# Gated linear attention and a cosine-gated MLP on one core: another hand-written order of the same steps

## The chip, the cores and the metric

One core of a Trainium2 chip runs the whole program. The metric is the device time of one execution in microseconds (us), the median of a few runs. The profiler recorded one execution; all times inside it count from the first instruction of the program.

## The reference

Four batches of eight heads, 768 positions, 48 values a head. A state of 48 x 48 decays row by row and takes an outer product at every position; the queries read it. The result, 3072 rows of 384, goes through a two-layer MLP whose hidden values are multiplied by their cosine.

```python
def _attn_ref(q, k, v, alpha):
    for t in range(S):
        state = alpha[:, :, t, :, None] * state + np.einsum('bhd,bhe->bhde', k[:, :, t], v[:, :, t])
        y[:, :, t] = np.einsum('bhd,bhde->bhe', q[:, :, t], state)

def _moe_ref(x, w_in, w_out):
    h = x @ w_in                       # 384 -> 2048
    g = h * np.cos(h)
    return (g @ w_out).astype(np.float32)
```

Inputs and output are float32.

## The kernel before

The work is cut into twelve blocks of 256 positions, called pairs here and `J` in the code (0 to 11); three pairs make a batch, and heads are taken two at a time. A pair holds even and odd positions apart (`e`) and two halves of 128 (`c`). Within a half the recurrence becomes products of matrices (scores under a mask), and the state passes from half to half. Every pair goes through these steps, and each step has one name in the plan:

- `load a`, `k`, `q`, `v`: one transfer of 384 KB each, on the queue of SyncE (SP). `w1` (two halves) and `w2` (four parts): the weights, cast to bf16 on their way, on the queue of GpSimd (POOL).
- `ln` (L142), on ScalarE (ACT): logarithms of alpha. `cums0`, `cums` (L156, L168), on TensorE (PE): running sums of them by products with triangles. From pair 3 on `mula` (L150, POOL) first joins two positions, and `sub` (L183, VectorE, DVE) gets the other sum.
- `icp`, `exps` (L193, L201), on ACT: exponentials of the sums and their inverses. From pair 3 on, `eb` does all four, and the logarithms of the next pair behind them: a session. Logarithm and exponential share one table of ACT's, the sine needs another, so a session among sines costs two table loads.
- `sk`, `sq` (L213, L217), on DVE or POOL: k and q times these exponentials. `castv` (L220, POOL). `vst` (L226, four DMAs) or, for pairs 0 to 2, `vpe` and `vev` (PE products, L235, and their evictions, L239): the values restacked.
- `trans` (L259, PE): 32 transposes into a PSUM tile `T_ps`. `evT 0`, `evT 1` (L265): its halves to SBUF, on DVE or ACT.
- `scores c` (L273, PE) and `mask c` (L278, DVE).
- `outer` (L290, PE), `add c` (L304, L306, DVE), `decay` and `state c` (L243, L312, POOL): the state.
- `yT` (L339, PE): the pair's output, transposed. `evy c` (L350, ACT or DVE): to SBUF as bf16.
- `m1 u` (L360, PE, u = 0 to 3): a quarter of the first projection, twelve products. `sin u` (L366, ACT): its cosine. `gate u` (L371, DVE): the two multiplied.
- `m2 c p` (L389, PE, p = 0 to 3): a quarter of the second projection of a half, four products. `evo c` (L401): its eviction. `out c` (L407): the store. The very last half is made in two columns (L383, L397).
- `idle` (L415): products of zeros, 41 in all, which keep PE running where it would stand.

PSUM has eight banks. One tile of one bank (`x`) serves `cums` and `vpe`, one (`o`) `m2` and `idle`, and three tiles of two banks (`h`) serve everything else: first sums, `T_ps`, scores, `outer`, `yT` and `m1`. A step that needs an `h` tile waits until the last reader of the oldest free one is done.

The order is written by hand. `PLAN` has a line for each step, with a number for each pair; the steps are sorted by that number and issued in this order, and every engine takes its own steps strictly in it. A letter behind the number picks the engine of a step: A is ACT, D is DVE; without one, scalings are on POOL, `evT` and `vev` on DVE, `evy` and `evo` on ACT. The numbers have no other effect: nothing waits for a time. `GATES` lets the load of alpha of pair 3 wait for pair 1's `yT`, and so everything behind it on SP.

```python
    for key, line in PLAN.items():
        kind, *rest = key.split()
        for J, word in enumerate(line.split()):
            if word != "-":
                t, _, eng = word.partition(":")
    with tc.manual_schedule():
        for _, _, kind, args in sorted(order, key=lambda x: x[:2]):
            steps[kind](*args)
```

Of the kernel before, what the change touches and what calls it, by code (L numbers as in the profile page):

```python
# [16 lines left out]
def kernel(  # L17
# [11 lines left out]
    B, H, S, D = q.shape  # L29
# [64 lines left out]
    w1 = [consts.tile([C, KT, DF // 2], BF, tag=f"w1{r}", name="w1") for r in range(2)]  # L94
    w2 = consts.tile([C, NF, DM], BF, tag="w2", name="w2")
# [315 lines left out]
    def idle(n):  # L411
# [18 lines left out]


    PLAN = {
        "load a": "750 2205 4425 24496 25066 37693 43693 45193 55293 56793 62293 70470",
        "load k": "3345 7425 31693 34693 40693 52193 64033 73545 85258 93648 94218 114101",
        "load q": "2775 8925 25636 36193 42193 52763 54533 63463 72180 78488 96723 113531",
        "load v": "5925 10425 33193 39193 46693 64693 71040 71610 94788 95358 117164 132675",
        "w1": "12930 13780 14800 45594",
        "w2": "18398 20198 24245 21048",
        "mula": "- - - 34028 35528 45595 55048 52028 70255 74420 95738 106328",
        "ln": "4660 6160 12304 35108 - - - - - - - -",  # L440
        "cums0": "5565 7065 13604 - - - - - - - - -",
        "cums": "5885 11199 13924 36668 44122 49975 61282 73275 86251 91443 105424 117024",
        "sub": "- - - 38162 44642 50732 65474 73795 87551 92648 106511 120780",
        "icp 0": "7285 8430 15799 - - - - - - - - -",
        "icp 1": "8805 11929 15424 - - - - - - - - -",
        "exps 0": "6900 7660 15039 - - - - - - - - -",
        "exps 1": "8045 13044 14654 - - - - - - - - -",
        "eb": "- - - 39444 47093 58049 68038 83323 88148 102153 108001 126061",
        "sk 0": "9160:D 14846:D 39112:D 41953:D 48949 58577 77428:D 89268 92888 110613 111733 130015",
        "sk 1": "9909:D 13739:D 38528 41528 47999 59591:D 73470 88318 91938 107448 124627:D 130965",  # L450
        "sq 0": "7660:D 15296:D 37028:D 43028 52978 60646:D 77878:D 84607 93838 103437 116334:D 127345",
        "sq 1": "8625 15746:D 37028 43028:D 54098 63884:D 70913:D 87368 90988 112683 109663 133792:D",
        "castv": "12160 17628 40028 46545 56778 71528 75880 90218 100558 104387 129245 144989",
        "vst": "- - - 48193 58293 82758 80258 91148 117734 111031 130175 145919",
        "vpe 0": "13195 20281 42879 - - - - - - - - -",
        "vpe 1": "15194 19341 41856 - - - - - - - - -",
        "vev 0": "13595:A 21966 43556:A - - - - - - - - -",
        "vev 1": "16174:A 19741:A 42256:A - - - - - - - - -",
        "decay": "14630 20028 36478 47315 53928 73300 73130 94788 107278 119391 111563 129075",
        "trans": "10624 16461 40648 44533 57020 68793 81884 90868 108663 115899 126133 137709",  # L460
        "evT 0": "11929 17161:A 42626:A 45233:A 60041 70290:A 83189 93123 109551 117529:A 130540:A 139589",
        "evT 1": "11324 18286 41348 46163:A 58511 71220:A 82584 91568 110631 116599:A 131821 138409:A",
        "scores 0": "14549 18771 45013 46729 68573 72307 85936 101052 116379 125693 140960 151870",
        "scores 1": "12159 19026 43154 48677 59649 82364 85716 101272 118725 125913 134675 140410",
        "mask 0": "16671 19211 46257 47397 69298 74270 86411 102140 116819 126133 144562 152310",
        "mask 1": "12599 20826 45117 49117 61096 84269 88026 105371 119165 127273 135115 140850",
        "outer": "14769 19786 41128 48897 68243 85386 81554 104346 116599 118945 140630 151540",
        "add 0": "16196 20351 44162 50257 68823 85936 82104 104896 117959 120305 141990 153450",
        "add 1": "17811 22813 - 51824 70438 - 83794 108126 - 121872 143557 -",
        "state 0": "16848 21898 44814 50909 69475 86588 82756 105548 118611 120957 142642 154102",  # L470
        "state 1": "19248 23465 - 55998 72350 - 94958 108778 - 128295 144209 -",
        "yT": "18046 23626 47792 56295 71422 88605 89395 107778 123407 138284 149254 161470",
        "evy 0": "19246 24739 49715 59116:D 72412 90700:D 90225:D 109076:D 125077:D 140194:D 150737 162583",
        "evy 1": "18876 25109 49345 58036:D 72782 89595:D 90795 110156:D 124397 139114:D 150367 162953",
        "m1 0": "22213 27478 51593 62900 74893 94379 97015 112527 128014 145205 157421 164967",
        "m1 1": "20895 30767 50275 64218 73575 93061 91743 120688 129985 146523 158739 168897",
        "m1 2": "26160 29449 52911 59964 78182 95697 102933 119370 133262 147841 153491 170215",
        "m1 3": "24842 34044 54229 61582 76211 98333 109238 111209 134990 143887 160057 171533",
        "sin 0": "23731 28996 53111 64418 76411 95897 98533 114045 129532 146723 158939 166485",
        "sin 1": "22413 32285 51793 65736 75139 94579 93261 122206 131503 148041 160257 170415",  # L480
        "sin 2": "27678 30967 54489 61595 79700 97215 105699 120888 134780 149359 155009 171793",
        "sin 3": "26360 37142 55747 63100 77729 99851 111547 112727 136508 145405 161575 173051",
        "gate 0": "24880 30145 54260 65949 78328 97046 99682 115194 130681 147872 160088 167634",
        "gate 1": "23562 33434 52942 67089 76288 95728 94410 123487 132652 149190 161406 171564",
        "gate 2": "28827 32116 55638 62744 80849 98364 106986 122347 136255 150508 156158 172942",
        "gate 3": "27509 39826 56896 64334 79468 101000 112696 113876 137657 146554 162724 174200",
        "m2 0 0": "28796 39247 55547 69368 82679 99651 110556 124292 136308 150139 162355 172851",
        "m2 0 1": "32085 39900 57595 70021 83332 100304 113845 124945 136961 150792 163008 174157",
        "m2 0 2": "32738 42131 58248 70674 83985 101587 114498 126708 139009 152185 163661 175463",
        "m2 0 3": "33391 43469 58901 72622 84638 102280 115151 127361 139662 152838 164314 176116",  # L490
        "m2 1 0": "35362 45328 65536 77529 86551 104771 117324 129332 141275 154809 166285 173504",
        "m2 1 1": "36015 45981 66189 79500 87204 105724 117977 131303 141928 155462 166938 174810",
        "m2 1 2": "36968 47044 66842 80153 87857 106377 122006 131956 142581 156115 167591 176769",
        "m2 1 3": "37621 49322 67495 80806 90120 107030 122659 132609 143234 156768 168244 177422",
        "evo 0": "34574:D 44322 62603 73475 85575 103280:D 116004 128413:D 140515 153925:D 165167:D 176969",
        "evo 1": "38637:D 54119 68348:D 81659 92173:D 108601:D 123512 133462 144087:D 157621 171423 178295:D",
        "out 0": "53933 66193 79058 75045 109831 110431 116564 149019 141075 173183 172583 177529",
        "out 1": "53333 62863 79658 98923 98223 109231 133245 148419 144717 158181 171983 178925",
    }
    IDLE = [(1201, 9), (6413, 2), (7383, 14), (11727, 1), (12377, 4), (15372, 5), (16939, 5), (20459, 1)]  # L500

    order = []
    for key, line in PLAN.items():
# [4 lines that stand above are left out]
                args = [J] + [int(x) if x.isdigit() else x for x in rest] + [{"A": "ACT", "D": "DVE", "P": "POOL"}[x] for x in eng]  # L508
                order.append((int(t), len(order), kind, args))
    for t, n in IDLE:  # L510
        order.append((t, len(order), "idle", [n]))
# [34 lines left out]
```

## Time and profile before

| what | us |
|---|---|
| median of 3 runs (183.7 to 184.37) | 184.28 |
| span of the profiled execution | 182.3 |
| PE busy | 175.4 |
| DVE busy | 134.8 |
| ACT busy | 129.9 |
| POOL busy | 71.4 |
| first quarter of the first projection begins | 21.30 |
| last product ends | 179.24 |

The time contains some 2 us that lie around the span. Busy time is the sum over an engine's instructions; matmuls overlap one another, so PE's share says that it seldom stands, not that it is at its peak. The largest groups on PE are the two projections (67.0 and 67.1 us), on DVE the gates (58.2 us), on ACT the cosines (53.3 us). ACT loads 18 tables of 1.28 us. Inputs are 12 x 4 transfers of 384 KB, in pieces under 512 bytes.

### The profile page before, as it was taken

The page shows a single profiled execution, that of the slowest core. Times are in us where ns is not written, and L with a number is a line of the kernel's source. Part 1 is how long each engine was busy: PE and PEld are TensorE (multiplying, and loading weights), DVE is VectorE, ACT ScalarE, POOL GpSimd, SP SyncE. Part 2 cuts the span into 40 slices and gives each one's busy share as a digit, 9 for nine tenths or more (in the row PEclk, how much of TensorE's full clock was granted, in tenths as well). Part 3 has the DMA queues.
Part 4 walks back from the last instruction along what each step waited for, and adds up shares of the span by engine and source line. Part 5 has one row for each costly group of instructions (what it writes and reads, how often), then busy time and mean ns, then how long its engine had stood idle before and what let it go on. Part 6 is the DMA issues. An engine that isn't in the chain of part 4 may idle for free.

```text
span 182.3 us, 5756 instructions
## 1 busy us (share of the span) xinstructions
PE 175.4 (96%) x2467; PEld 132.6 (73%) x2470; DVE 134.8 (74%) x183; ACT 129.9 (71%) x169; POOL 71.4 (39%) x104
## 2 busy tenths in 40 slices
PE   7999899989999999998999999999999999999993
PEld 2455789746697877975799669686876796787872
DVE  7188878678879897599889886978688778363460
ACT  2837687998989999959578999838964174383331
POOL 5145830377777103734894298240720320100000
PEclk9999999999999999999999999999999999999999
DMA  5999999999989959996629905690052142010032
GB/s 148 261 261 220 199 215 221 273 260 265 248 184 283 249 132 295 289 277 202 147 63 229 273 18 166 155 233 0 4 110 83 45 109 81 4 43 4 0 129 86
DMA packets 57801, 29.47 MB, mean 162 GB/s; under 512 B 50992, under 2 KB 56496, under 8 KB 57776
## 3 DMA queue, kind: packets, MB, share of 16 engines
q1 hardware_dynamic: 56256, 25.86, 58.3%
q0 software_dynamic: 1376, 3.15, 9.3%
q8 instruction: 19, 0.31, 0.7%
q10 hardware_dynamic: 144, 0.10, 0.2%
q14 instruction: 6, 0.05, 0.1%
HBM read 25.17 MB, written 4.72 MB: 164 GB/s over the span
## 4 chain that ended last, share of the span: by engine, by line
PE 77%; ACT 11%; DVE 6%; DMA 2%; issue 2%; ACTq 0%
PE h_ps L360 29%; PE o_ps L389 28%; PE y_ps L339 5%; DVE gsb L371 5%; PE idle_ps L415 4%; ACT c_sb L366 3%; PE A_ps L273 3%; PE T_ps L259 3%; DMA a<-in_alpha_dram 2%; PE U_ps L290 2%; ACT L366 2%; PE o_last L383 1%; ACT L137 1%; ACT lna L142 1%; PE cums_h L156 1%
## 5 line engine op out<-in xcount | busy, mean ns | idle before, releaser
L371 DVE TENSOR_TENSOR gsb<-h_ps,c_sb 128x1024 bf16<-128x1024 f32 x48 | 58.2, 1222 | 20.8 <-ACT c_sb L366 19.4
L366 ACT ACTIVATE c_sb<-h_ps,halfpi 128x1024 bf16<-128x1024 f32 x48 | 53.3, 1115 | 26.7 <-PE h_ps L360 26.4
L389 PE MATMUL o_ps<-w,gsb 128*128 128x384 bf16 x368 | 67.1, 327 | 0.6 <-DVE o_sb L401 0.6
L360 PE MATMUL h_ps<-xT,w 128*128 128x256 bf16 x576 | 67.0, 273 | 0.3 <-issue 0.2
L360 PEld LDWEIGHTS <-w 128*128 128x128 bf16 x576 | 62.4, 114 | 2.5 <-DMA w<-in_moe_w_in_dram 0.3
L389 PEld LDWEIGHTS <-gsb 128*128 128x128 bf16 x368 | 33.9, 98 | 21.4 <-issue 1.1
L312 POOL TENSOR_TENSOR un<-us,c 128x384 bf16<-128x384 f32 x20 | 16.8, 838 | 46.2 <-DVE us L304 36.9
L278 DVE TENSOR_TENSOR A_sb<-A_ps,msk 128x1024 bf16<-128x1024 f32 x24 | 28.9, 1216 | 3.4 <-PE A_ps L273 3.4
L217 POOL TENSOR_TENSOR qh<-q,cp 128x384 bf16<-128x384 f32 x13 | 13.8, 1063 | 13.3 <-ACT cp L201 12.2
L213 POOL TENSOR_TENSOR kh<-k,icp 128x384 bf16<-128x384 f32 x15 | 14.9, 1007 | 2.4 <-ACT icp L193 1.0
L220 POOL CAST vp<-v 128x768 bf16<-128x768 f32 x12 | 9.9, 827 | 12.0 <-DMA v<-in_v_dram 12.0
L150 POOL TENSOR_TENSOR a<-a 128x384 f32<-128x384 f32 x9 | 9.0, 1003 | 10.1 <-DMA a<-in_alpha_dram 10.1
L142 ACT ACTIVATE lna<-a 128x768 bf16<-128x768 f32 x12 | 10.1, 844 | 3.5 <-DMA a<-in_alpha_dram 3.3
L415 PE MATMUL idle_ps<-zeros 128*128 128x512 bf16 x38 | 11.1, 439 | 1.4 <-DVE halfpi L77 1.2
L401 ACT COPY o_sb<-o_ps 128x384 f32<-128x384 f32 x13 | 6.2, 478 | 8.5 <-PE o_ps L389 8.5
L137 ACT ACT_TABLE_LOAD x9 | 11.5, 1283 | 0.9 <-PEq L530 0.7
L366 ACT ACT_TABLE_LOAD x9 | 11.5, 1283 | 0.2
L304 DVE TENSOR_TENSOR us<-U_ps,un 128x384 f32<-128x384 f32 x16 | 8.8, 551 | 3.8 <-POOL un L312 2.1
L265 ACT COPY qkT<-T_ps 128x1024 bf16<-128x1024 bf16 x10 | 9.8, 1016 | 1.9 <-PE T_ps L259 1.8
L217 DVE TENSOR_TENSOR qh<-q,cp 128x384 bf16<-128x384 f32 x11 | 6.8, 629 | 5.4 <-DMA q<-in_q_dram 5.3
L265 DVE COPY qkT<-T_ps 128x1024 bf16<-128x1024 bf16 x14 | 9.4, 680 | 1.2 <-PE T_ps L259 1.2
L273 PE MATMUL A_ps<-qkT 48*128 48x128 bf16 x192 | 9.0, 217 | 0.7 <-DVE gsb L371 0.5
(70 smaller groups left out, 156.6 us busy)
## 6 DMA issues: line engine op xcount, KB each, us to landing
a<-in_alpha_dram SPq DMA_DIRECT2D x12, 384.0 KB, 5.9
q<-in_q_dram SPq DMA_DIRECT2D x12, 384.0 KB, 6.1
k<-in_k_dram SPq DMA_DIRECT2D x12, 384.0 KB, 6.0
v<-in_v_dram SPq DMA_DIRECT2D x12, 384.0 KB, 6.3
out_dram<-o_sb SPq DMA_DIRECT2D x23, 192.0 KB, 3.5
vs<-vp SPq DMA_DIRECT2D x36, 64.0 KB, 2.8
w<-in_moe_w_in_dram POOLq DMA_DIRECT2D x2, 768.0 KB, 9.6
w<-in_moe_w_out_dram POOLq DMA_DIRECT2D x4, 384.0 KB, 8.7
```

What stands on the lines that cost most here:

```text
L137: nc.scalar.preload_act_table_set("natural_log_exp_and_others")
L213: eng.tensor_tensor(out=kh_t[J % NQ][:, e, :, 0:D], in0=kqv["k", J][:, :, e], in1=icp_, op=ALU.mult)
L217: eng.tensor_tensor(out=qh_t[J % NQ][:, e, :, 0:D], in0=kqv["q", J][:, :, e], in1=cp, op=ALU.mult)
L265: copy(out=qkT_sb[J][:, c], in_=T_ps[J][:, c].rearrange("r n e s -> r n (e s)"))
L273: nc.tensor.matmul(A_ps[J, c][:, a, p, :], qkT[r, c, NP + p, :], qkT[r, c, p, :], start=True, stop=True)
L278: nc.vector.tensor_tensor(out=A_sb[J][:, c].rearrange("s a p t -> s (a p) t"), in0=A_ps.pop((J, c)).rearrange("s a p t -> s (a p) t"), in1 ...
L312: nc.gpsimd.tensor_tensor(out=u, in0=U_sum.pop(n), in1=c2_sb[J][:, :, c].unsqueeze(3).to_broadcast([C, NP, 2, D]), op=ALU.mult)
L360: nc.tensor.matmul(h_ps[J, u][:, f, :], cols, xT[J][:, kk, :], start=(kk == 0), stop=(kk == KT - 1))
L366: nc.scalar.activation(out=c_sb[J, u], in_=h_ps[J, u], func=AF.Sin, bias=halfpi, scale=1.0)
L371: nc.vector.tensor_tensor(out=gsb[J][:, u * FW : (u + 1) * FW], in0=h_ps.pop((J, u)), in1=c_sb.pop((J, u)), op=ALU.mult)
L389: nc.tensor.matmul(o_ps[J, c][:, 0:DM], gsb[J][:, ft, c * C : (c + 1) * C], w2[:, ft], start=(ft == 0), stop=(ft == NF - 1))
L415: nc.tensor.matmul(idle_ps[0], zeros[:, 0:C], zeros, start=True, stop=True)
```

## The change

Every number in `PLAN` is new, in steps of ten, and so is the order on each engine. Nothing outside `PLAN` and `IDLE` is touched; there are as many instructions of each kind on PE, and the same transfers. What differs:

- Scalings (`sk`, `sq`): 20 were on DVE and 28 on POOL, now 11 and 37.
- Evictions. `evT`: 14 on DVE and 10 on ACT, now 17 and 7. `vev`: 1 and 5, now 3 and 3. `evy`: 10 and 14, now 12 and 12. `evo`: 11 and 13, now 9 and 15 (each with the last, which is cut between both).
- ACT loads 16 tables instead of 18.
- The products of zeros stand in seven places instead of eight: 22 in front of the first sums, where 9 were.
- SP starts with alpha of pair 1, then alpha of pair 0, v, k, q; it was alpha of pair 0, of pair 1, q, k. q and k of pair 2 now come ahead of alpha of pair 3.
- On POOL's queue the second half of `w1` and the parts of `w2` stand behind more scalings.
- The first eight quarters `m1` (pairs 0 and 1) have no `m2` between them; before, four `m2` stood among them.

The start of PE's order, before:

```
idle x9 | cums0 0 | cums 0 | idle x2 | cums0 1 | idle x14 | trans 0 | cums 1 | idle x1 | scores 1 of 0 | idle x4 |
vpe 0 of 0 | cums0 2 | cums 2 | scores 0 of 0 | outer 0 | vpe 1 of 0 | idle x5 | trans 1 | idle x5 | yT 0 |
scores 0, 1 of 1 | vpe 1 of 1 | outer 1 | vpe 0 of 1 | idle x1 | m1 1, 0 of 0 | yT 1 | m1 3, 2 of 0 | m1 0 of 1 | m2 0 0 of 0 | m1 2, 1 of 1 | m2 0 1, 0 2, 0 3 of 0 | m1 3 of 1
```

and after:

```
idle x22 | cums0 0 | cums 0 | cums0 1 | cums 1 | vpe 0 of 0 | idle x8 | outer 0 | vpe 1 of 0 | trans 0 | cums0 2 | cums 2 |
idle x4 | scores 0, 1 of 0 | trans 1 | idle x7 | scores 1 of 1 | yT 0 | vpe 1 of 1 | scores 0 of 1 | outer 1 | vpe 0 of 1 |
m1 1 of 0 | yT 1 | m1 0, 2 of 0 | m1 1, 2, 3 of 1 | m1 3 of 0 | m1 0 of 1 | m2 0 0, 0 1, 0 2, 0 3 of 0
```

The diff, cut to the lines that the text speaks of (the columns are pairs 0 to 11):

```diff
-        "load a": "750 2205 4425 24496 25066 37693 43693 45193 55293 56793 62293 70470",
+        "load a": "30 20 120 1200 1230 1550 1620 2080 2920 2270 3550 2860",
...
-        "w1": "12930 13780 14800 45594",
-        "w2": "18398 20198 24245 21048",
+        "w1": "370 620",
+        "w2": "970 900 930 1010",
...
-        "sk 0": "9160:D 14846:D 39112:D 41953:D 48949 58577 77428:D 89268 92888 110613 111733 130015",
-        "sk 1": "9909:D 13739:D 38528 41528 47999 59591:D 73470 88318 91938 107448 124627:D 130965",
-        "sq 0": "7660:D 15296:D 37028:D 43028 52978 60646:D 77878:D 84607 93838 103437 116334:D 127345",
-        "sq 1": "8625 15746:D 37028 43028:D 54098 63884:D 70913:D 87368 90988 112683 109663 133792:D",
+        "sk 0": "270 420:D 1250 1590:D 2250 2590:D 3180 3410 3920 4720 5190 5390",
+        "sk 1": "240:D 540 1210 1600 2280 2330 3150 3380:D 3910 4530 5400 5350",
+        "sq 0": "260:D 590 960 1850:D 2300:D 2650 2960:D 3530 3940:D 4810 5180 5580",
+        "sq 1": "320 600:D 1030 1800 2140 2420 3250 3560 3900 4940 5240 5730",
...
-        "evT 0": "11929 17161:A 42626:A 45233:A 60041 70290:A 83189 93123 109551 117529:A 130540:A 139589",
-        "evT 1": "11324 18286 41348 46163:A 58511 71220:A 82584 91568 110631 116599:A 131821 138409:A",
+        "evT 0": "480 680 1500 1940:A 2410 2950 3320:A 3870 4350 5070:A 5570 5800:A",
+        "evT 1": "520:A 660:A 1380 1910 2470 3010 3460 3850 4450:A 5150 5690 5790",
...
-        "m1 0": "22213 27478 51593 62900 74893 94379 97015 112527 128014 145205 157421 164967",
-        "m1 1": "20895 30767 50275 64218 73575 93061 91743 120688 129985 146523 158739 168897",
+        "m1 0": "990 1190 2040 2380 3090 3950 3990 4790 5320 5820 6170 6310",
+        "m1 1": "840 1070 2010 2630 3070 3790 3890 4620 5370 5610 6130 6370",
...
-        "m2 0 0": "28796 39247 55547 69368 82679 99651 110556 124292 136308 150139 162355 172851",
+        "m2 0 0": "1240 1690 2320 2750 3340 4080 4540 5050 5600 5960 6350 6580",
...
-    IDLE = [(1201, 9), (6413, 2), (7383, 14), (11727, 1), (12377, 4), (15372, 5), (16939, 5), (20459, 1)]
+    IDLE = [(10, 1), (40, 15), (90, 6), (250, 1), (280, 7), (460, 4), (630, 7)]
```

## The prediction

> **What bounds the kernel now.** I read the page's busy times and slices first, then what TensorE (PE) waited for, then the timeline of the first 25 us, because a new order can win only where PE stands still.
>
> ```profile
> span 182.3 us, 5756 instructions
> ...
> PE   7999899989999999998999999999999999999993
> ...
> DMA  5999999999989959996629905690052142010032
> ```
>
> PE is busy in every slice, the DMA engines in the first eleven (50 us). The chain of waits goes through PE for nearly the whole span:
>
> ```profile
> 0.74 3.92 DMA a<-in_alpha_dram
> ...
> 21.30 1.49 PE h_ps L360 x12
> ...
> 177.91 1.33 PE o_last L383 x16
> ```
>
> Columns: start, us, what. The first projection `m1` starts at 21.30, the last product ends at 179.24. The list of PE's own waits is short:
>
> ```profile
> PE o_ps L389 <- DVE o_sb L401: 0.6, 1, 0.6
> PE A_ps L273 <- DVE gsb L371: 0.5, 1, 0.5
> ```
>
> These two (at 38.7 and 82.6) and about 0.2 at 117.4 are all the standing after 25 us: 1.3 us. Everything later than that is PE work which both orders contain, with 42 changes from second-projection parts to something else in either. So a better middle can win at most 1.3 us, and the start, where PE fills its time with products of zeros, decides. I therefore walk the start with the rows below.
>
> ```profile
> 13.79 1.03 DVE L213 TENSOR_TENSOR kh<-k,icp 128x384 bf16<-128x384 f32 x2
> ...
> 15.26 1.03 DVE L217 TENSOR_TENSOR qh<-q,cp 128x384 bf16<-128x384 f32 x2 [0.43 <-DMA q<-in_q_dram]
> ...
> 15.38 0.88 ACT L193 ACTIVATE icp<-cums_h 128x384 f32<-128x384 f32 x2
> ...
> 16.64 0.41 PE L259 MATMUL T_ps<-ident_bf,kh 64*128 64x64 bf16 x16
> 16.67 1.21 DVE L278 TENSOR_TENSOR A_sb<-A_ps,msk 128x1024 bf16<-128x1024 f32 x1
> ...
> 17.33 1.01 ACT L265 COPY qkT<-T_ps 128x1024 bf16<-128x1024 bf16 x1 [0.70 <-PE T_ps L259]
> ```
>
> The seventh load (k of pair 1) is in by 13.79, the eighth (q of pair 1) by 15.26: 1.5 us each, since the first landed at 4.67. From the first transpose to its eviction on ScalarE (ACT) is 0.69 (16.64 to 17.33). Operations in a row on ACT or VectorE (DVE) overlap by some 0.08, as the pairs show (two in 0.88).
>
> **The change, part by part.** Same products, same tiles, same transfers: only orders and engines move.
>
> *The zeros.* Twenty-two of the 41 now stand ahead of the first running sums instead of nine. The rows space the first nine by 0.427 and the later ones by 0.213. With full speed from about 6.1 as before, eleven run slowly from 1.2 and eleven fast: done at 8.3. The first alpha is now second in the queue (6.2 instead of 4.67), its logarithm ready at 7.05. So the sums start at 8.3 rather than 5.6. What hides this: nothing of pair 2's session on ACT can run before its alpha lands, sixth as its neighbours show (12.25; the sixth load's user waited until then), and ACT has done the six earlier exponentials by 11.8 (9.3 + six of 0.42). Without that cover it would cost 2.7.
>
> *The start's critical chain.* The seventh load is the same one and still lands at 13.79, but more hangs on it in series:
> - DVE: scaling of k (0.56) and the first eviction of pair 0's transposes (0.66), which the new order puts behind it: 15.0. Before, pair 0's transposes were evicted at 11.2 to 12.5.
> - ACT: the other half's eviction, waiting for DVE's since both write one tile: 15.05 to 16.06.
> - PE scores to mask 0.46, mask 1.21: 17.77. (DVE has the q scaling, landed 15.26, done by 16.05.)
> - Pair 1's transposes: their PSUM buffer is the one whose scores that mask reads, so they wait for it: 17.8, plus 0.69, plus eviction 1.01 on ACT: 19.52. Behind it on ACT stand pair 2's two inverse exponentials (0.88): 20.35. They free the buffer of pair 0's output product `yT`.
> - `yT` to its eviction 0.86 (18.40 to 19.26 in the trace): 21.26; its halves are evicted one on ACT (0.60), the second on DVE after it (0.59): 22.5. The first projection follows at 22.6, where before it began at 21.30: **+1.3**.
>
> On PE itself the steps before it end at 22.6 to 22.85 (two value stackings around ACT's eviction of the first), so 1.3 to 1.5.
>
> *The next eight projections.* DVE goes on with add 0.55, mask 1.21, value eviction 0.55, add 0.55 before pair 1's `yT` can end (25.3). Then all eight `m1` come in a row without a second-projection part between. Three PSUM buffers serve them, and one is freed late: gate 1 of pair 0 is through at 26.5, its neighbour's eviction on DVE at 27.0, ACT's at 27.65, then sine 1.11 and gate 1.22 end at 29.95, while PE is ready at 29.2: a wait of 0.8. The eight end at 35.2. Before, the same eight and four parts `m2` (0.65 each) ended at 35.87, which is 33.27 without them: **+1.9** in all for the start. Its bounds: the scaling at 13.79 came right behind a mask (12.45 to 13.66), so that load may have landed as early as the sixth, 12.3; then ACT's value eviction (14.5) holds the chain, 0.6 sooner, +1.3. If no two operations overlap, seven more times 0.08, +2.5. I take +1.9, by the even spacing of the landings.
>
> *Weights.* The first half of `w1` is issued on GpSimd (POOL) behind the scalings of pair 0, at 12.9 (before 13.0), and lands at 21. The second, now behind two scalings of pair 1, is issued at 16.4 instead of 13.9; since the first occupies the queue for 4 us anyway, it lands at 25.0 as before, wanted at 26.6. The four parts of `w2` are issued from 23.9 to 29.1 instead of 18.4 to 25.0. At 1.95 us each (0.77 MB in the 4 us from 16 to 20) plus 2.2 from issue to first byte and 1.7 to landing, the third and last land at 34.3 and 36.2, wanted at 35.2 and 37.1. Cover 0.9; if it is gone I allow up to 0.8 in the range. It rests on how the engines share:
>
> ```profile
> q0 software_dynamic: 162, 0.45, 90.4%
> q1 hardware_dynamic: 161, 0.06, 13.8%
> ```
>
> This is 28.5 to 31 us (packets, MB, share of the engines): the two queues moved as many packets, but the weights' (q0) are 2.8 KB and the inputs' 0.4 KB, so weights got nearly all of it. The Trainium skill (DMA: Bandwidth & Descriptors, "Anatomy of one DMA — SWDGE (gpsimd) path") fits a DMA issued from GpSimd with 2.0 us plus its bytes at 436 GB/s. By that a part of `w2` would be there 2.9 us after its issue, the cover would be 4 us, and the third rival below impossible; the trace's 0.77 MB in 4 us is less than half that rate, and it decides.
>
> Two loads of pair 2 (q, k) now go ahead of the wait for pair 1's `yT` on SP's queue; they finish by 26, in the gap of the weights, and nothing needs them before 26.8.
>
> *Engines.* POOL gets 9 scalings more (1.0 us each in place of 0.65 on DVE); DVE loses 9 of these and two output evictions, and gains 3 transposes' evictions (0.68), 2 of values and 2 of `xT`: some 3 us less. ACT loses 3 transposes' evictions (1.02), 2, 2 and a pair of table loads (2.6), gains 2 outputs: 7 us less. POOL at 71.4 has room. None is the bound over the span, so I price these at nothing; the cover is PE's own work, and where it is missing the next part counts it.
>
> *The middle.* An exponential session on ACT is the longest stretch that PE must cover:
>
> ```profile
> 56.84 1.28 ACT L137 ACT_TABLE_LOAD   x1
> 58.13 0.52 ACT L193 ACTIVATE icp<-cp 128x384 f32<-128x384 f32 x1
> ...
> 59.72 0.84 ACT L142 ACTIVATE lna<-a 128x768 bf16<-128x768 f32 x1
> ```
>
> That is 1.6 for four exponentials (58.13 to 59.72), 0.75 for the logarithm, 1.28 for the way back. The tightest place in the new order is pair 4's session: after ACT's transposes' eviction of pair 3 it runs 1.6 + 0.75 + 1.28, two sines 2.1, a gate 1.2, hand-overs 0.15: 7.1, before the third `m1` of pair 2 finds a buffer. PE has two scores 0.67, three `m1` 3.93, sums 0.33, `m2` 0.65, `yT` 0.73: 6.3 to 6.6 with changes. Wait 0.5. Pair 3's logarithm keeps the sums 0.3, pair 4's transposes 0.1. In all 0.9, and I allow 0.7 more for waits that such sums don't find (those at 82.6 and 117.4 are of that kind). Minus the 1.3 that go: **+0.3**. The tail is the same eight parts behind the last `m1`; gate 3 (2.55 us behind it) is in time for the fifth part (2.6).
>
> **Sum.** 182.3 + 1.9 + 0.3 = 184.5 of span. The median of 184.28 lies 2.0 over the span: **186.5 us**, 1.2% slower. Its own range is 185.3 to 188.
>
> **Rivals.**
> 1. *ACT and DVE fall behind in every session.* If operations in a row don't overlap in the new mixture, a session is 4 x 0.50 + 0.84 + 1.28 + 1.12 + 1.22 = 6.5 against 5.6 of PE work, 0.9 short, in five sessions (pairs 4 to 8) 4.5 us: 186.2 + 4.5 = 190.7. For it: ACT is at 34.4 of 36 us from 36 to 72. Against: the overlaps are in the trace. Chance 0.18.
> 2. *The stock covers everything* (the other side). The eight `m1` in a row put off pair 0's `m2`, so from 37 us on one pair more of parts is in stock whenever an engine is late. If it covers all, neither the 0.9 nor the 0.7 arises: 184.28 + 1.9 - 1.3 = 184.9, and with the start at its lower bound 184.3: not slower by what can be told. It decides if PE's list of waits is empty after 36 us. Against: the parts stand in a fixed order, and PE can't take one early. Chance 0.18.
> 3. *The weights come late.* If inputs got as many bytes as weights, a half of `w1` would take 7.7 us (landing 24.5, 1.9 late) and the last `w2` about 4 more: 192.5. Against: 0.45 to 0.06 MB above. Chance 0.05.
> 4. *The clock falls* in a pause of the start (PE waits from 16.6 to 17.8). Products then cost double (0.427 to 0.213), for some 2 us of the chain's work: 188.5. Against: the granted clock is 9 in every slice, and the old start pauses too (0.5 at 13.0). Chance 0.03. The Trainium skill (TensorE: Matmul & The Clock Gate, "Part 1: The HAM clock gate") says that the clock halves after an idle window of about 3.4 us; by that this rival adds nothing, since no pause of the chain is as long, and no run here has one.
>
> **Numbers.** Forecast 0.52; 0.04 stay for gains that no row here shows. What a measurement of this kernel can tell from no change is about 0.5%, 183.4 to 185.2. Slower: 0.47 of the forecast, rivals 1, 3 and 4 (0.26), 0.05 of rival 2: 0.78, with rounding. Same: 0.05 of the forecast and 0.13 of rival 2, less 0.01: 0.17. Faster: the rest, 0.05. Range: from between rival 2's two times to a little over rival 1's, 184.5 to 191.
>
> **What would show it.** Right: first `m1` at 22.6 to 22.9, with pair 0's transposes evicted behind a DVE scaling at 13.8; eighth `m1` done near 35.2; a wait of 0.8 on a gate before the fourth; table loads 16; PE waits after 36 us of about 1.6. Wrong: a first `m1` by 21.5; PE waiting for DMA `w` at 35 to 39; or waits after 36 us of 4 us and more, with ACT before them.

## The result, and the profile after

| | before | after |
|---|---|---|
| time, median | 184.13 | 192.09 (four runs, 190.38 to 192.54) |
| span of the profiled execution | 182.3 | 190.3 |
| first `m1` starts | 21.30 | 27.64 |
| the first eight `m1` end (before: without the four `m2` between) | 33.27 | 40.4 |
| last product ends | 179.24 | 186.44 |
| from there to the end of the span | 3.1 | 3.9 |

The changed kernel is slower by a ratio of 1.042 (95% interval 1.0375 to 1.0465). A ratio compares the means of two kernels without the runs that took over 1.5% more than the kernel's fastest, so it can differ from the quotient of two medians. Of the 8.0 us of span, 7.1 are there when the first eight `m1` are done, 0.1 come between 40 us and the last product, and 0.8 behind it. The page's head and two rows of its slices:

```profile
span 190.3 us, 5757 instructions
...
PE   7993799899999999999999999999999999999991
...
PEclk9999579999999999999999999999999999999999
```

A slice is 4.8 us. PE is down to 3 and 7 in the fourth and fifth, and the granted clock, 9 throughout before, is 5 and 7 in the fifth and sixth (19 to 28 us). The timeline of the changed kernel shows why (start, duration, engine, line, operation, and in brackets how long the engine stood before it and what ended that):

```profile
12.82 0.93 POOL L125 DMA_DIRECT2D w<-in_moe_w_in_dram  x1
...
13.60 3.51 DVE L213 TENSOR_TENSOR kh<-k,icp 128x384 bf16<-128x384 f32 x1 [0.53 <-DMA k<-in_k_dram]
...
13.78 0.85 POOL L312 TENSOR_TENSOR un<-us,c 128x384 bf16<-128x384 f32 x1
...
14.57 0.22 POOL L243 TENSOR_TENSOR c<-cp,dmask 128x16 f32<-128x16 f32 x1
14.75 0.99 POOL L213 TENSOR_TENSOR kh<-k,icp 128x384 bf16<-128x384 f32 x1
15.70 0.98 POOL L217 TENSOR_TENSOR qh<-q,cp 128x384 bf16<-128x384 f32 x1
...
18.23 0.40 PE L273 MATMUL A_ps<-qkT 48*128 48x128 bf16 x8 [2.68 <-DVE us L304]
...
21.50 3.17 PE L415 MATMUL idle_ps<-zeros 128*128 128x512 bf16 x7
```

The seventh load is in at 13.60, as forecast. The scaling that waits for it takes 3.51 instead of 0.56, and ends 0.43 behind POOL's fourth operation in a row (16.68); none of POOL's four is longer than usual. Everything behind it on DVE is late by that, PE stands 2.68 and, ahead of pair 1's transposes (20.53), 1.32 more; then the clock falls, and seven products of zeros take 3.17, 0.45 each instead of 0.21.

The page of the kernel before already held the sign. This is the answer on line 213 there (shortest, median and longest duration in ns):

```profile
L213 POOL TENSOR_TENSOR kh<-k,icp x15: 994/1005/1027, 38.7 to 132.4; 128x384 bf16<-128x384 f32 x15
L213 DVE TENSOR_TENSOR kh<-k,icp x9: 546/618/905, 9.3 to 125.6; 128x384 bf16<-128x384 f32 x9
```

The same shape takes 546 or 905 on DVE. Laid over POOL's timeline, each long one begins while POOL multiplies, and ends 0.42 behind that operation (42.07 to 42.97 beside POOL's 41.56 to 42.56). The prediction took its price from the two at 13.79, which ran while POOL issued transfers and multiplied nothing. From the timeline of the kernel before:

```profile
13.02 1.72 POOL L125 DMA_DIRECT2D w<-in_moe_w_in_dram  x2
...
41.56 1.00 POOL L213 TENSOR_TENSOR kh<-k,icp 128x384 bf16<-128x384 f32 x1 [0.70 <-ACT cp L201]
...
42.07 0.91 DVE L213 TENSOR_TENSOR kh<-k,icp 128x384 bf16<-128x384 f32 x1
```

### The profile page after: what moved, and what is told of

Same layout as the page of the kernel before. It is cut to its first block, busy times and chain, and to the rows that moved or that the text cites. A ratio compares the mean times of both kernels' runs of the same rounds, so it can differ in the third digit from the quotient of the medians.

```text
span 190.3 us, 5757 instructions
## 1 busy us (share of the span) xinstructions
PE 178.6 (94%) x2470; PEld 134.5 (71%) x2470; DVE 135.4 (71%) x179; ACT 123.5 (65%) x162; POOL 80.2 (42%) x113
## 4 chain that ended last, share of the span: by engine, by line
PE 63%; ACT 16%; DVE 9%; DMA 3%; SPq 3%; issue 3%; DVEq 0%
PE h_ps L360 27%; PE o_ps L389 24%; ACT c_sb L366 4%; PE y_ps L339 3%; DMA k<-in_k_dram 3%; SPq L105 3%; DVE gsb L371 3%; PE A_ps L273 2%; PE T_ps L259 2%; ACT L366 2%; ACT L137 2%; ACT qkT L265 2%; DVE A_sb L278 2%; ACT cp L201 2%; PE idle_ps L415 2%
## 5 line engine op out<-in xcount | busy, mean ns | idle before, releaser
L360 PE MATMUL h_ps<-xT,w 128*128 128x256 bf16 x576 | 67.9, 273 | 1.1 <-DVE gsb L371 0.9
L213 POOL TENSOR_TENSOR kh<-k,icp 128x384 bf16<-128x384 f32 x19 | 19.2, 1026 | 4.2 <-ACT icp L193 3.6
L217 POOL TENSOR_TENSOR qh<-q,cp 128x384 bf16<-128x384 f32 x18 | 18.4, 1024 | 3.9 <-DMA q<-in_q_dram 3.8
L401 ACT COPY o_sb<-o_ps 128x384 f32<-128x384 f32 x15 | 7.2, 479 | 12.4 <-PE o_ps L389 12.4
L415 PE MATMUL idle_ps<-zeros 128*128 128x512 bf16 x41 | 13.1, 485 | 1.2 <-DVE zeros L52 1.2
L350 ACT CAST xT<-y_ps 128x384 bf16<-128x384 f32 x12 | 6.8, 594 | 11.0 <-PE y_ps L339 7.3
L265 ACT COPY qkT<-T_ps 128x1024 bf16<-128x1024 bf16 x7 | 7.1, 1011 | 9.1 <-DVE qkT L265 7.0
L265 DVE COPY qkT<-T_ps 128x1024 bf16<-128x1024 bf16 x17 | 11.4, 681 | 2.0 <-ACT qkT L265 1.9
L273 PEld LDWEIGHTS <-qkT 48*128 48x128 bf16 x192 | 6.0, 95 | 7.3 <-DVE us L304 3.2
L213 DVE TENSOR_TENSOR kh<-k,icp 128x384 bf16<-128x384 f32 x5 | 6.5, 1300 | 6.0 <-ACT icp L193 5.5
```

Of the source, the lines that this page charges most:

```text
L213: eng.tensor_tensor(out=kh_t[J % NQ][:, e, :, 0:D], in0=kqv["k", J][:, :, e], in1=icp_, op=ALU.mult)
L217: eng.tensor_tensor(out=qh_t[J % NQ][:, e, :, 0:D], in0=kqv["q", J][:, :, e], in1=cp, op=ALU.mult)
L265: copy(out=qkT_sb[J][:, c], in_=T_ps[J][:, c].rearrange("r n e s -> r n (e s)"))
L273: nc.tensor.matmul(A_ps[J, c][:, a, p, :], qkT[r, c, NP + p, :], qkT[r, c, p, :], start=True, stop=True)
L360: nc.tensor.matmul(h_ps[J, u][:, f, :], cols, xT[J][:, kk, :], start=(kk == 0), stop=(kk == KT - 1))
L415: nc.tensor.matmul(idle_ps[0], zeros[:, 0:C], zeros, start=True, stop=True)
```

## The experiments

Theory: a DVE operation with both inputs in SBUF stands still while POOL works on SBUF, and the pause that this made took the clock down.

**The collision by itself.** The kernel before, with scratch work behind its last product:

```
+ for dve in (two SBUF inputs, one, one of two in PSUM):
+     for pool in (0, 4):          # POOL multiplications beside it
+         arm(dve x2, pool)
```

> The kernel before with scratch work behind its last product: pairs of DVE operations of 128x384 with two f32 inputs in SBUF, with one, and with one of the two inputs in PSUM, each once with POOL idle and once beside four POOL multiplications of the same size (about 1.0 us each). Theory (a DVE operation with both inputs in SBUF stands still while POOL works on SBUF): 0.56 each with POOL idle; beside POOL the first of the pair takes at least 1.0 more, up to the whole stretch of POOL, 3 us; the PSUM kind stays within 0.1 of its time alone; for the one-input kind it says nothing. Rival (the long scaling was its own load landing late or in pieces): every pair takes the same beside POOL as alone, 0.56 each.

The timeline of this run; x2 is the pair of DVE operations, x4 POOL's four:

```profile
180.94 1.15 DVE L536 TENSOR_TENSOR md<-mx,my 128x384 bf16<-128x384 f32 x2
...
182.42 4.59 POOL L531 TENSOR_TENSOR mp<-mx,my 128x384 bf16<-128x384 f32 x4 [27.40 <-DVE mx L529]
182.91 2.18 DVE L536 TENSOR_TENSOR md<-mx,my 128x384 bf16<-128x384 f32 x2
...
195.96 1.15 DVE L538 TENSOR_TENSOR md<-m_ps,mb 128x384 bf16<-128x384 f32 x2
```

1.15 alone, 2.18 beside POOL, and 1.15 beside POOL with an input in PSUM: the collision is there, and only for inputs in SBUF. Copies with one SBUF input went from 0.76 to 1.85. But DVE came in after one POOL operation each time, and POOL paid too (4.59 against 4.20). One collision costs 0.4 to 0.7 (0.92 and 1.23 for the two of the pair, instead of 0.56), not 2.95: the theory is right in kind and short in size.

**Three edits of the start.** Pair 1's two scalings back on DVE; only the issues of `w1` moved; only zeros added.

```
undo_pair1   "sk 1" J1: 540 -> 540:D     "sq 0" J1: 590 -> 590:D
w1_between   "w1": "370 620" -> "505 510"
zeros        IDLE: (460, 4) -> (460, 16), and (605, 7) added
```

> The changed kernel with the two scalings of pair 1 that it gave to POOL (k of half 1, q of half 0) back on DVE; POOL keeps the state of pair 0 and the small product for the decay beside the k scaling at 13.6. Theory (POOL's work stops the scaling): it lasts only until these two end, 1.2 to 1.7 us instead of 3.51, the first m1 starts at 24.0 to 25.7 instead of 27.64, the time is 187.5 to 190. Rival A (k of pair 1 itself is late): 3.5 us and 191.5 to 192.5. Rival B (the fallen clock did it alone): scaling 3.5, first m1 at 27.

> The changed kernel with all its engines; only the issues of the two halves of w1 on POOL are moved: from ahead of the state of pair 0 and behind the scalings of pair 1 to between the two, so that POOL issues transfers (14.0 to 16.0) while DVE scales k, and scales later. Theory (only POOL's work on SBUF stops DVE): the k scaling takes 0.6 to 1.4 us, the q scaling on DVE becomes the long one (1 to 2 us) beside POOL's scalings, first m1 24.5 to 26.5, time 188 to 191. Rival C (POOL's issuing of transfers stops DVE): the k scaling takes 2.4 us or more. Rival A (k late): 3.5.

> The changed kernel with 19 more products of zeros where PE stood still at 15.5 to 18.2 (12) and ahead of pair 1's transposes (7), nothing else. Theory (the clock fell because PE stood still, and this is the second part of the loss): the k scaling stays at 3.5, the granted clock stays at 9 in every slice, the seven zeros behind the transposes take 1.5 instead of 3.1, first m1 at 25.0 to 26.0, time 189.3 to 190.8. Rival (the clock costs nothing, the chain on DVE and ACT is all): first m1 27 to 28, time 191.5 or more.

*undo_pair1*: 191.88 (ratio 1.043, 1.037 to 1.050): nothing won, where 187.5 to 190 was expected. The scaling took 1.20, as the theory said, so k was not late and the clock was not the cause (rivals A and B fall). But the q scalings, now two on DVE, took 2.28 instead of 1.01 beside POOL's state and cast of v (15.95 to 18.1), 1.18 and 1.17 with one POOL operation each; PE stood 2.8 ahead of the transposes, the clock fell, and the first `m1` came at 26.97, where 24.0 to 25.7 was expected. The collision had moved to the next operation.

*w1_between*: 189.55 (1.031, 1.0275 to 1.0345). Its timeline on DVE:

```profile
13.83 0.55 DVE L213 TENSOR_TENSOR kh<-k,icp 128x384 bf16<-128x384 f32 x1
...
15.58 1.21 DVE L217 TENSOR_TENSOR qh<-q,cp 128x384 bf16<-128x384 f32 x1
```

With every engine as in the changed kernel, and only the work beside it another, the k scaling is back at 0.55, and the first `m1` at 24.07, 3.6 sooner, although it waited 0.65 for weights issued later. Part of the 0.55 is luck: in this run the 22 zeros took 7.88 instead of the changed kernel's 7.04, so that POOL's state came late (14.06) and began 0.23 behind the scaling. In *clear* below, where no issue stands ahead of the state either, the state began first and the scaling took 1.06. The q scaling of 1.21 lay beside two issues and not, as expected, beside scalings; I have no cause for it.

*zeros*: 190.54 (1.037, 1.033 to 1.0415). The scaling is as long as before (3.55), the clock 9 in every slice, and the first `m1` at 25.41. So the fallen clock was worth 2.2 us at the first `m1` and 1.5 of the medians (the intervals of the two ratios overlap); some 1.0 was given back at 41.6, where PE stood for a logarithm.

**The start with POOL out of the way.** All four scalings of pair 1 on DVE, the first half of `w1` behind the state (370 -> 505), and

```
+ if n == 1:   # second state of pair 0, on POOL
+     tc.add_manual_dep(op.ins, HOLD[1].ins.name, ...)   # waits for pair 1's transposes
```

> The changed kernel with all four scalings of pair 1 on DVE, the first half of w1 issued behind the state of pair 0, and POOL's next work on SBUF (the second state of pair 0 and what follows it) made to wait for pair 1's transposes, so that POOL hardly touches SBUF while DVE scales. Theory (the two operations shared the way to SBUF, and the pause this made took the clock down; nothing else is wrong with the new start): scalings of 0.55 each but for up to 0.6 on the first, granted clock 9 throughout, first m1 at 22.8 to 23.8, time 186.3 to 188.0. Rival (the new order of the start has another loss of its own): first m1 behind 24.5, time 189 or more.

The same with the nine zeros of the kernel before ahead of the first sums, (40, 15) -> (40, 2); and with zeros added where PE stood, (460, 4) -> (460, 5) and (605, 7); and that with `w1` issued at 370 again:

> The same with nine products of zeros ahead of the first running sums instead of 22. Theory (the 22 are covered by the wait for the sixth and seventh load): the first running sums start a microsecond earlier, first m1 and time as in that kernel within 0.5 us. Rival (the zeros delay the start): 1 us or more faster. If the clock is not up without them: slower by 1 or more.

> The kernel with the cleared start (all scalings of pair 1 on DVE, POOL kept off SBUF, the first half of w1 issued later) with eight more products of zeros, one at 15.5 and seven ahead of pair 1's transposes, where PE stood 1.55 us. Theory (what is left of its loss in most runs is the clock, which fell in that pause): granted clock 0.99 to 1.0 in every run, first m1 at 23.0 to 23.8, time 186.5 to 187.8 in every run. Rival (the clock does not hang on these pauses): times from 187 to 191 as without the zeros.

> The cleared start with the added zeros, but with the issues of both halves of w1 where the changed kernel has them, so that no product waits for weights. Theory (what the new start costs without POOL in DVE's way, with the clock up and the weights in time): the k scaling 0.9 to 1.3, no wait for w, granted clock 0.99 or more, first m1 at 22.8 to 23.4, eighth m1 done at 35.3 to 36.0, time 187.0 to 189.0 (of the 4.5 us won at the first m1 up to 1.2 were given back later in the other runs). Rival (the issue ahead keeps DVE out again): k scaling 3 us, time 190 or more.

*clear*: 189.17 (1.026, 1.0205 to 1.031), in the median the rival's time. But two of its six runs had the clock at 1.0 and took 187.25 and 187.27, as the theory said; four, at 0.99, took 189.1 to 190.9. In the one with a profile, of these four, PE stood 1.55 ahead of the transposes, the seven zeros behind took 2.58 instead of 1.68, and the first `m1` came at 24.48. *clear_few*: 189.65, sums at 6.88 instead of 8.23, first `m1` at 24.45: the 22 zeros in front cost nothing (its clock fell in front as well, but the k scaling began at 13.57, as in *clear*). *clear_zeros*: clock 0.997 to 1.0 in all six runs, but 189.73, where 186.5 to 187.8 was expected: PE was ready for the first `m1` at 22.78 and then waited 1.17 for the half of `w1` that I had moved behind the state. *clear_w1*: 188.37 (1.022, 1.019 to 1.0255), no wait for `w1`, first `m1` at 23.38, the eighth done at 36.1, then 0.6 of waiting for `w2`. Its k scaling took 1.45, since it met POOL's state again; without these 0.89 PE would have been ready for the first `m1` at 22.5 (an estimate), though the first half of `w1` landed at 23.1.

**Why four in a row.** Here POOL's multiplications write four tiles, so that none waits for another; then a transfer is issued ahead of them.

```
port2   POOL: mul mul mul mul          DVE: two at once, or beside issues alone
port3   POOL: issue mul mul mul mul    DVE: one, started at five places
```

> The kernel before with scratch work behind its last product, as in the first measurement of this kind, but POOL's four multiplications write four separate tiles, so that none waits for the one before. Theory (DVE gets the shared path only where POOL leaves a gap): beside them the pair of DVE operations with two inputs in SBUF takes at least 3.5 us (1.15 alone, 2.18 beside a chain in which each waited for the last); with one input in PSUM 1.15. Rival (DVE waits for the one POOL operation that runs, and then goes): 2.0 to 2.4 again. Third part: four such DVE operations beside the issue of two transfers of weights by POOL (1.7 us): 2.2 if issuing does not stop DVE, about 2.9 or more if it does.

> The kernel before with scratch work behind its last product: five times POOL issues one half of w1 (about 0.9 us) and then multiplies four separate tiles (1.0 each), while DVE starts one operation with two inputs in SBUF ahead of the issue, or 0.3 to 0.9 into it. Theory X (an operation of DVE that is started while POOL issues a transfer loses its turn, and is kept out until POOL's row of operations ends, as the one of 3.51 in the changed kernel): at least one of the four later starts takes 4 us or more. Theory Y (POOL gives way after one operation, as in the two measurements before, and the 3.51 has a further condition): 0.55 where it ends before the multiplications begin, else at most 1.5.

*port2*: the pair took 2.25, the theory's 3.5 did not come; beside issues alone four took 2.34. *port3*: the four later starts took 4.58, 4.10, 3.71 and 3.98, each ending 0.42 behind the last multiplication. The first of them in its timeline:

```profile
188.24 0.81 POOL L125 DMA_DIRECT2D w<-in_moe_w_in_dram  x1 [0.31 <-issue]
188.74 4.58 DVE L538 TENSOR_TENSOR md<-mx,my 128x384 bf16<-128x384 f32 x1
189.06 3.84 POOL L533 TENSOR_TENSOR mp<-mx,my 128x384 bf16<-128x384 f32 x4
```

An issued transfer in front of the row makes the difference: with it, DVE gets in only when POOL stops. What stands behind it was then varied.

```
port4   issue+2 mul; issue+4 (late start); issue+4 (two on DVE); mul+issue+3; 4+issue; issue+issue
port5   issue+mul+small; the same+issue; issue+mul+small+2 mul+issue; issue+2 mul+issue;
        issue+mul+small+2 mul; issue+small+2 mul
```

> The kernel before with scratch work behind its last product, to find how long a row of POOL work behind an issued transfer keeps out a DVE operation with two inputs in SBUF. Six parts, DVE started 0.4 into the first POOL operation: issue and two multiplications; issue and four, DVE started in the second of them; issue and four, with two DVE operations; one multiplication, issue, three more; four multiplications and then an issue; two issues alone. Theory X (once a transfer was issued, POOL does not give way until it has nothing to do): 0.42 behind the last multiplication in parts 1 to 3 (about 2.6, 3, 4.1 and then 0.55) and in part 4 either after the first multiplication (0.9) or 0.42 behind the last; part 5 at most 1.5, part 6 0.55 (1.2 if the long q scaling beside two issues in an earlier run was of this kind). Theory Z (it takes a row of four): part 1 at most 1.5.

> The kernel before with scratch work behind its last product: one DVE operation with two inputs in SBUF, started 0.6 into POOL's issue of a transfer; behind the issue stand on POOL: a multiplication (1.0 us) and a small one (0.2); these and another issue; these, two more multiplications and an issue (the changed kernel's row); two multiplications and an issue; a multiplication, a small one and two multiplications; a small one and two multiplications. Theory (a second issue behind the row, close by, lets DVE in after the first operation): parts 1, 3, 5, 6 end 0.42 behind the last multiplication, parts 2 and 4 0.42 behind the first. Rival (the small operation lets it in, if nothing large stands behind it): parts 1 and 2 end 0.42 behind the first multiplication, all others 0.42 behind the last.

*port4*: behind an issue, two multiplications kept DVE out 2.56, and four kept out one that began in the second (2.81) and the first of two (4.51, the second 0.56). With the issue second in the row, DVE asked 0.14 before the end of the first multiplication and was done during the issue (0.56), ahead of the three that followed, so this part says nothing on them; with the issue last it got in behind the first multiplication (0.56, and POOL's next took 1.32); two issues alone: 0.56, so the 1.21 above isn't explained by them. *port5*, two parts of its timeline:

```profile
183.85 1.61 DVE L544 TENSOR_TENSOR md<-mx,my 128x384 bf16<-128x384 f32 x1
184.03 1.50 POOL L540 TENSOR_TENSOR mp<-mx,my 128x384 bf16<-128x384 f32 x2
...
204.08 3.72 DVE L544 TENSOR_TENSOR md<-mx,my 128x384 bf16<-128x384 f32 x1
204.30 3.07 POOL L540 TENSOR_TENSOR mp<-mx,my 128x384 bf16<-128x384 f32 x4
```

Behind an issue, one multiplication and the small one let DVE in after the first (1.61, with another issue behind 1.75), but the changed kernel's own row (large, small, large, large) kept it out to the end, 3.72; the other rows with two large operations did so too (2.67, 3.78, 2.56). The rival's reading held, and it fits the kernels: out to the end in the changed one, in after the state in *undo_pair1* and *clear_w1*, whose row is state and small product. The row has to follow the issue at once: in *undo_pair1* POOL stood 0.33 between its second issue and the state and cast behind it, and DVE was in after each (the 1.18 and 1.17 above). Why an issue does this no run shows.

**The same change in the old order**, and **the last stores**:

```
old_pool2    before: "sk 1" J1: 13739:D -> 13739     "sq 0" J1: 15296:D -> 15296
tail         after: "out 0" J11: 6730 -> 6705 (ahead of "out 1" J11, 6720)
clear_tail   clear_w1 with the same
```

> The kernel before with the two scalings of pair 1 that the change gave to POOL (k of half 1, q of half 0) given to POOL, all orders kept. There POOL stands free around 14, so DVE's scaling at 13.8 starts first and POOL's waits for it, not the other way round. Theory (place decides, not the engine by itself): DVE's scalings 0.55 to 0.7, transposes of pair 1 up to 0.6 later, time 184 to 185. Rival (two more scalings on POOL in the start cost what they seem to cost in the changed kernel): first m1 3 us later or more, 187 or more.

> The changed kernel with one number altered: the store of pair 11's first half (192 KB) stands ahead of its second half's on SP's queue again, as in the kernel before, instead of behind it. Theory (the change put the larger store last, and that is 0.8 us which the prediction did not see): from the end of the last product to the end of the span 3.0 to 3.2 instead of 3.9; time 191.0 to 191.8. Rival (the last stores overlap whatever their order): 3.8 to 3.9 and 192.

> The cleared start with the zeros added and w1 issued where the changed kernel has it, and the two last stores in the old order. Theory (what stands between the prediction's 186.5 and this start's 188.4 is 0.8 of the last store, 0.9 of the k scaling that still meets one POOL operation, the rest a wait for w2): span 186.5 to 186.8, time 187.3 to 187.9. Rival (the last store hides): span 187.4, time 188.2 to 188.6.

*old_pool2*: 183.60 against 183.65 (ratio 0.9999, 0.9985 to 1.0012). The k scaling did meet POOL's (1.46, not 0.55 to 0.7), and the first `m1` still began at 21.33: the old order had room there. The place costs, not the engine.

The stores show in the timeline of the changed kernel's end (DMA_DIRECT2D: a transfer is issued):

```profile
186.44 0.36 DVE L397 COPY o_half<-o_last 128x192 f32<-128x192 f32 x1 [2.90 <-PE o_last L383]
...
186.82 0.33 SPq L407 DMA_DIRECT2D out_dram<-o_half  x1
187.25 0.40 SPq L407 DMA_DIRECT2D out_dram<-o_sb  x1
```

`o_sb`, twice as large and ready earlier, is issued last, 0.43 behind the halves; before it went at 178.45, ahead of them. With the old order of the two, the span ends 3.1 behind the last product in both kernels (3.9 without). The medians don't resolve it: *tail* 190.68 over runs from 188.28 to 193.12, *clear_tail* 189.03 against 188.37. The profiled run of *clear_tail* took 192.29: at 98.4 PE stood 3.05 for nothing that its trace shows, and the granted clock was 0.58 from 101 to 104, so not every fallen clock comes from the start.

The profiled run of *tail* (188.28) gave one thing more. Its start is the changed kernel's, but its 22 zeros took 6.31 instead of 7.04, so the sums and POOL's row came 0.7 sooner, and POOL reached its scaling of q of pair 1 just before that load landed (15.12):

```profile
13.71 1.79 DVE L213 TENSOR_TENSOR kh<-k,icp 128x384 bf16<-128x384 f32 x1 [1.37 <-DMA k<-in_k_dram]
...
14.09 0.99 POOL L213 TENSOR_TENSOR kh<-k,icp 128x384 bf16<-128x384 f32 x1
15.19 1.17 POOL L217 TENSOR_TENSOR qh<-q,cp 128x384 bf16<-128x384 f32 x1
```

POOL stood for 0.1 at 15.08, DVE came in there, the scaling took 1.79, the clock held, and the first `m1` was at 23.57 instead of 27.64. The loss hangs on a tenth of a microsecond, which would explain why this kernel's runs lie so far apart (not tried). No version of the new start beat the kernel before.

## Why the prediction missed

- **The step that failed** is the first of "The start's critical chain": "DVE: scaling of k (0.56)". It took 3.51, +2.95. Behind it stands "Engines", where nine more scalings on POOL were priced at nothing because none was the bound; four POOL operations of pairs 0 and 1 stood just there. The runs put the collision in place of that price: *w1_between* took it away (0.55; 1.06 in *clear*, where the state began first), and *port5* made it anew (3.72). The Trainium skill (SBUF — State Buffer, "Who interferes with whom") has the rule that the prediction overlooked: a VectorE operation with two inputs in SBUF and a GpSimd operation that reads SBUF exclude each other for a whole instruction. The runs agree for POOL's single operations; that a row behind an issued transfer counts as one is more than it says, and it doesn't account for DVE's losing although it began 0.18 ahead of POOL.
- **Rival 4, the clock**, came in as a consequence, worth 2.2 at the first `m1` (*zeros*) where 2 were priced, with a chance of 0.03. Its chance was wrong because the pause was taken as 1.2, and because the Trainium skill's rule (TensorE: Matmul & The Clock Gate, "Part 1: The HAM clock gate") of an idle window of about 3.4 us was read as a safe bound. Here the clock fell after stands of 2.68 and 1.32 with 1 us of work between them, and in *clear* after 1.55 (profiled in one of the four runs with the lower clock). The old start's pause of 0.5 at 13.0, which spoke against this rival, isn't in the trace: behind its first products PE's longest stand there is 0.37, at 5.2.
- **The rest of the chain was right**: *clear_zeros* had PE ready at 22.78 and *clear_w1*, less its scaling's 0.89, at 22.5, against 22.6. The changed kernel's own start, in the profiled run of *tail*, gives 22.3 (23.57 less the 1.23 that its scaling took too long). From the first `m1` to the eighth's end 12.6 were forecast, and 12.7 came in both *clear_w1* and the changed kernel. The +1.9 of the start itself therefore stands: 1.9 + 2.95 + 2.2 is the 7.1 found.
- **The zeros** cost nothing, as said (*clear_few*).
- **Weights** came later than forecast. The first half of `w1` took 10.2 from issue to landing (8.0 before) and landed at 23.0 instead of 21, the second at 27.5 instead of 25.0; a first `m1` at 22.6 would have stood 0.4 for them. The cover of 0.9 for `w2` was gone where the start was nearly as fast as forecast: 0.6 of waiting in *clear_w1*. In the changed kernel itself the late start hid both. So rival 3 (the weights come late) came in part. Two loads of pair 2 now go on beside `w1`: from 16 to 20 us the weights' queue moved 0.58 MB beside 0.33 of inputs, where it moved 0.77 alone before. No run left these loads out.
- **The middle**: +0.3 forecast, +0.1 found. PE's stands behind 40 us sum to 1.3, the largest 0.43 at 61.1, where 1.6 was forecast and 1.3 stood before. So rival 1 did not come, and rival 2 (the stock covers everything) neither: it wanted an empty list.
- **The tail** was called the same; the moved store made it 0.8 longer, a step that the prediction didn't list.

Over the forecast span of 184.5 that is 2.95 + 2.2 + 0.8 - 0.2 = 5.8, and 190.3 was found. The profiled run of *clear_w1* (span 187.4) lies 2.9 over the forecast span: 0.9 of the k scaling, 0.6 of the wait for `w2`, 0.8 of the last store, and 0.6 at 98.6, where PE stood for nothing that the trace shows. That 0.6 stays open.

## What to carry to other kernels

Before a DVE operation is priced from its group, look at the group's longest, and lay each long one over POOL's timeline: two inputs in SBUF beside busy POOL is another price. When work goes to POOL, ask what DVE does in that microsecond on the critical chain, and above all whether an issued transfer with several POOL operations right behind it stands there. A pause that such a stall makes costs a second time through the clock, so cover PE's pauses near 1.5 us with products of zeros, and give the last place on the store queue to the smallest store.

## What the runs showed of the hardware

- Behind an issued transfer POOL did not let DVE in between its operations: 2.6 to 4.6 for an operation of 0.56, ending 0.42 to 0.43 behind POOL's last in eleven of eleven scratch rows with two or more large operations right behind the issue. With one large and one small operation it was in after the large one (1.61, 1.75), and where POOL stood 0.33 behind the issue, after one of two (*undo_pair1*). Without the issue DVE was in after one in the scratch runs (0.9 to 1.3).
- DVE copies with one SBUF input (f32 to bf16) are hit as well: 0.36 each alone, 0.78 and 1.04 beside POOL.
- One input in PSUM makes an operation immune: 1.15 a pair in both cases.
- The granted clock fell after pauses of PE of 2.7 and 1.3 us in short order (the changed kernel), of 2.8 (*undo_pair1*) and of 1.55 (*clear*, *clear_few*), and held after 1.44 (*w1_between*).
- The same 22 products of zeros at the start took 6.31 (*tail*), 7.04 (the changed kernel) and 7.88 us (*w1_between*).
